# VectorE turns q and k of three more pairs, TensorE masks part of the second batch, and slots no longer go two by two

## The chip, the cores and the metric

One NeuronCore of a Trainium2 chip runs the whole program. The metric is the device time of one execution in microseconds (us): the kernel before takes 1088.77 us, the median of three runs (1088.58 to 1090.57).

## The reference

Two blocks follow each other. First a block-sparse attention over 4 batches, 8 heads, 768 positions, head size 64:

```python
scores = scale * np.matmul(q, k.transpose(0, 1, 3, 2))
# mask in blocks of 32: neighbours, first and last block, and three sampled blocks per row of blocks
scores = np.where(mask, scores, -1000000000.0)
attn = softmax(scores)                  # max subtracted, sum + 1e-9
attn_out = np.matmul(attn, v)           # (B, H, S, D) -> x of (B, S, H*D) = (4, 768, 512)
```

Then a Fourier mixing layer with a channel network (512 to 2048 to 512):

```python
X = np.fft.fft(np.fft.fft(x, axis=1), axis=2)
u = x + np.real(X)
un = (u - mean(u)) / np.sqrt(var(u) + 1e-06)
return u + np.maximum(un @ w_ch1, 0.0) @ w_ch2
```

Everything is fp32.

## The kernel before

**Attention in units and slots.** Heads go in pairs: 16 pairs `n`, four to a batch, `NP = 4`. A pair has two halves of 384 queries and six chunks of 128 keys, so twelve *units* (half, chunk). Two units make a *slot*: six slots to a pair, 24 (`SB`) to a batch, 96 in all. Below, slots are counted from 0, so the second batch has slots 24 to 47.

For a unit, `scores` (L536) multiplies on TensorE (L551): two matmuls of 64 rows, one for each head, into one of two PSUM tiles `s`. In the first batch two more matmuls (L559) add the mask as a product of two bf16 factors, `of_k` and `off_q`. `weigh` (L563) takes the exponential on ScalarE: in the first batch straight from `s` to `e` (L569); later in place in `s` (L572), and VectorE multiplies by a 0/1 mask of bytes on the way to `e` (L574). There are four `e` buffers. From the second batch on GpSimd adds the `e` of a half up in `acc` (L584), from which TensorE makes the softmax sums once per pair (`total`, L677); in the first batch TensorE does it for each slot (`add_up`, L663). `values` (L587) multiplies by v (L597).

**Turning q and k.** Both have to have the head dimension on the partitions. In `turn` (L472) TensorE transposes 12 tiles a pair (L486) and ScalarE copies them out of PSUM (L489, L495). From pair `BY_VECTOR` on, `load_blocks` brings q and k in blocks of 32, VectorE turns them (`flip_blocks`, L520) and ScalarE puts q in order (`in_order`, L528). The loads go through SyncE's queue.

**The mixing layer.** Once a batch has its attention, `begin` (L1251) lines up its steps: `before` and `after`, a long chain of small steps through VectorE (scaling L705, folds L728 to L756, arrivals L855, normalisation L866 to L880), TensorE (`zp`, `pq`, `utp`) and ScalarE, kept in `apart`; and `rest`, the *channels* (`quad` L992 and `channels` L1048), 155.6 us of TensorE work per batch by the planner's numbers, which go to `late` when the chain is through.

**The order.** Each engine runs its instructions in the order in which the program issues them, and the whole order is written by a planner in the program: `when` holds its guess of each engine's time, and `slot` (L1271) issues scores, exponentials, values, then steps of the mixing layer where `gap` (L1215) finds that they would be ready, then channels at a pace that keeps 100 us (`COVER`) of them back for the next batch's chain. The planner sums its own constants (0.9 us for a scaling, for instance), not measured times.

A batch's tiles are reused two batches later, so `until` at slot 53 empties `late` of the first batch before the third batch writes its first result.

When `late` is not empty at an even slot, `paired` is set for good: the sums of two slots are held back in `due`, and the order becomes scores, four units' values, scores, channels.

Of the kernel before, what the change touches and what calls it, by code (L numbers as in the profile page):

```python
# [12 lines left out]
BF16 = mybir.dt.bfloat16  # L13
# [4 lines left out]
ALU = mybir.AluOpType  # L18
# [84 lines left out]
def kernel(  # L103
# [14 lines left out]
    nc = tc.nc  # L118
# [73 lines left out]
    def busy(engine, us, after=0.0):  # L192
        when[engine] = max(when[engine], after) + us
        return when[engine]
# [14 lines left out]
    loaded, v_of = {}, {}  # L209


    BY_VECTOR = 2 * NP + 1

    def load_blocks(n, a, tile):

# [219 lines left out]
    def room(i, shape, name, dtype=FP32):  # L435
        return big.tile(shape, dtype, tag=f"big{i}", name=name)
# [29 lines left out]

    turned, e_of, acc_of, o_of, sums_of, x_of, sp_of = {}, {}, {}, {}, {}, {}, {}
    s_at, e_at, oT_at, acc_at = {}, {}, {}, {}  # L470

# [64 lines left out]
    def scores(us):  # L536

        n, w = divmod(us[0], UP)
        half = w // C
        qT, kT = turned[n, 0], turned[n, 1]  # L540
        queries = slice(half * HS, (half + 1) * HS)
        got = []
        for u in us:
            c = u % C
            s = ps_s.tile([P, 2, 512], FP32, tag="s", name="s")
            got.append((u, s))
            busy("PE", 0.72, max(e_at.get(u - SLOT, 0.0), z_at[u % 2]))
            s_at[u] = when["PE"] + HOP
            for i in range(2):
                rows = slice(D * i, D * i + D)  # L550
                nc.tensor.matmul(s[:, i, 0:HS], kT[rows, c * P:(c + 1) * P], qT[rows, queries],  # L551
                                 start=True, stop=n >= NP)
        for u, s in got if n < NP else ():
            c = u % C
            busy("PE", 0.25)
            s_at[u] = when["PE"] + HOP
            for i in range(2):
                rows = slice(D * i, D * i + D)
                nc.tensor.matmul(s[:, i, 0:HS], of_k[rows, c * P:(c + 1) * P], off_q[rows, queries],  # L559
                                 start=False, stop=True)  # L560
        return got

    def weigh(u, s):  # L563
        n, w = divmod(u, UP)
        half, c = divmod(w, C)
        e = ep.tile([P, 2, HS], FP32, tag="e", name="e")
        e_of[u] = e
        if n < NP:
            nc.scalar.activation(out=e, in_=s[:, :, 0:HS], func=ACT.Exp, scale=scale)  # L569
            e_at[u] = busy("ACT", 0.8, s_at[u]) + HOP  # L570
            return
        nc.scalar.activation(out=s[:, :, 0:HS], in_=s[:, :, 0:HS], func=ACT.Exp, scale=scale)  # L572
        m = mask[:, c, half * HS:(half + 1) * HS].rearrange("p (o s) -> p o s", o=1)
        nc.vector.tensor_tensor(out=e, in0=s[:, :, 0:HS], in1=m.broadcast_to([P, 2, HS]),  # L574
                                op=ALU.mult)
        e_at[u] = busy("DVE", 0.97, busy("ACT", 0.8, s_at[u]) + HOP) + HOP
        if c > 0:
            acc_at[n, half] = busy("POOL", 2.0, e_at[u]) + HOP
        if c == 1:
            acc_of[n, half] = acc_p.tile([P, 2, HS], FP32, tag="acc", name="acc")  # L580

        for i in range(2 if c > 0 else 0):
            acc = acc_of[n, half][:, i, :]
            nc.gpsimd.tensor_add(out=acc, in0=e_of[u - 1][:, i, :] if c == 1 else acc,  # L584
                                 in1=e[:, i, :])
# [601 lines left out]
    SP = UP // SLOT  # L1187
    SB = SP * NP
    W_PACE = 1.42
    short, apart, late, due = deque(), deque(), deque(), deque()  # L1190
    state = {"paired": False, "w": 0, "got": 0, "owed": 0.0, "ready": 0.0}

    def channel_step():
        late.popleft()[0]()
# [20 lines left out]
    def gap(rest=0.0, ahead=None, kinds="tm"):  # L1215

        used = "".join(k for k in "tm" if k not in kinds)
        if ahead is None:
            ahead = AHEAD if late else ALONE
        while apart:  # L1220
            kind, fn, pe, act, dve, need = apart[0]
            if len(late) > need:
                break
            if kind in "dw":
                if kind == "w" and rstd_at[0] > max(when["DVE"], when["PE"]) + 0.2:
                    break
                if max(when["DVE"], state["ready"]) + dve > when["PE"] + rest + ahead:
                    break
            elif kind != "-":
                bank_at = (max if kind == "M" else min)(free[kind.lower()])  # L1230
                if kind.lower() in used or max(state["ready"], bank_at) > when["PE"] + 0.1:
                    break
                used += kind.lower()
            do_apart()
        for item in list(short):
            kind, ready, fn = item
            if kind not in used and max(ready, min(free[kind])) <= when["PE"] + 0.1:
                used += kind
                short.remove(item)
                fn()  # L1240
# [10 lines left out]
    def begin(b):  # L1251


        before, after, rest = mixer(b, x_of[b, 0], x_of[b, 1])
        any_of = len(late) + len(apart) + 4 * len(rest)
        hold = 2 * T
        apart.extend((*step, any_of) for step in norm_steps(b) + before)
        apart.extend((*step, hold) for step in after)
        apart.append(("-", lambda: late.extend(rest), 0.0, 0.0, 0.0, hold))

    def w_loads():
        while state["got"] < min(len(wchunks), state["w"] + ROOMS):
# [3 lines left out]
    def w_steps(sl):  # L1266
        while state["w"] < min(len(wchunks), W_PACE * sl):
            w_round(state["w"])
            state["w"] += 1

    def slot(sl):  # L1271
        phase, r = divmod(sl, SB)
        n, s = divmod(sl, SP)
        units = range(SLOT * sl, SLOT * sl + SLOT)
        opens = sl % 2 == 0
        state["paired"] |= opens and len(late) > 0
        paired = state["paired"]

        def sum_up():

            at = due.popleft()
            done = range(SLOT * at, SLOT * at + SLOT)
            for u in done:
                values(u)
            if at < SB:
                add_up(done)
            for u in done:
                e_of.pop(u)

        if paired and len(due) == 2 and due[0] % SP % T == T - 1:
            sum_up()
        got = scores(units) if sl < B * SB else ()
        if paired and len(due) == 2:
            sum_up()
        for u, ps in got:
            weigh(u, ps)
        if not paired and not late:  # L1300
            gap(1.5)
        while due and (opens or not paired):
            sum_up()
        due.append(sl)
        if s == (4 if paired else 3) and n + 2 < len(pairs):
            load_q(n + 2)
        if s == 0 and 0 < n < len(pairs) - 1:
            load_k(n + 1)

        reuse = n % NP == 0 and phase >= 2  # L1310
        if sl > 0 and s == (5 if reuse else 4 if paired else 3) and sl <= B * SB:
            b, j = pairs[n]
            at = oT_at[n, 0]
            if reuse:
                until(lambda: (b - 2, 0) in finished)
                at = when["PE"] + LEAVES
            if in_blocks(n):
                place_blocks(n, 0)
            else:
                short.append(("t", at, lambda: place(n, 0)))  # L1320
# [12 lines left out]
        if sl > SB and s == 0 and sl <= B * SB:  # L1333
            short.append(("t", acc_at[n - 1, 1], lambda: total(n - 1)))
        if n + 1 < len(pairs):
            for at, a, half in ((1, 0, 0), (2 if n > 0 else 3, 0, 1),
                                (3 if paired else 4, 1, 0), (5, 1, 1)):
                if s == at and n + 1 < BY_VECTOR:
                    short.append(("t", 0.0, lambda a=a, half=half: turn(n + 1, a, half)))
            if s == 1:  # L1340
                load_v(n + 1)
# [9 lines left out]
        us = sum(step[1] for step in late)  # L1351
        pace = max(LEAST, min(MOST, (us - COVER) / left)) if left > 0 else MOST
        state["owed"] = min(state["owed"], pace) + pace if late else 0.0
        more = paired and opens and sl < B * SB
        if not more:
            gap(max(state["owed"], 0.0))
        while not more and late and state["owed"] >= late[0][1] / 2:
            state["owed"] -= late[0][1]
            channel_step()
            gap(max(state["owed"], 0.0))  # L1360

        must = (3, 5) if paired else (2, 5)
        while short and (not more or r == 0) and (s in must or len(short) > 1 or phase == 0 or r == 0):
            ready = [i for i in short if max(i[1], min(free[i[0]])) <= when["PE"] + 0.1]
            if not ready and s not in must and r > 0 and sl > 1:
                break
            item = ready[0] if ready else short[0]
            short.remove(item)
            item[2]()
# [5 lines left out]
                    fn(*args)  # L1375
        w_loads()
        w_steps(sl)
        if sl >= 4 and sl % 2 == 0:
            table_step()

# [139 lines left out]
```

## Time and profile before

| | |
|---|---|
| median of three runs | 1088.77 us |
| the profiled execution | 1088.58 us, of which the span from first to last instruction is 1086.9 us |
| TensorE matmuls | 1046.6 us busy |
| VectorE | 683.2 us |
| ScalarE | 380.1 us |
| GpSimd | 271.0 us |
| granted TensorE clock | 0.992 of full speed, mean |

Lines are those of the kernel as printed above. PE is TensorE's matmul, PEld its weight load, DVE VectorE, ACT ScalarE, POOL GpSimd, SP SyncE; a `q` behind a name is that engine's sequencer. A line of the timeline has the start, the duration, the engine, the line, the operation, what it writes and reads with shapes, the count that was merged, and in brackets how long the engine stood idle before it and who released it. An fp32 matmul leaves two records, so a slot's scores are `x8`. A matmul's duration in the records covers its own pipeline; the step from one start to the next tells better what it costs TensorE.

### The profile page before, as it was taken

Reading aid. Unit: us, or ns where it says so; the run is one execution under the profiler, and the core shown is the slowest. Engines: PE = TensorE matmul, PEld = TensorE weight load, DVE = VectorE, ACT = ScalarE, POOL = GpSimd, SP = SyncE. Lnnn points to the kernel's source line nnn. Section 1 sums busy time; section 2 is a strip of 40 time slices with the busy share of each in tenths; the row PEclk is TensorE's granted clock in tenths of the full one; section 3 lists DMA queues with packets and bytes.
Section 4 is the critical chain, followed back from the end, with each engine's and each line's share of the span. In section 5 each row is a group of like instructions: output and inputs, shape, how many; then the busy total and the mean of one; then the engine's idle time right before and its main releaser. Section 6 shows DMA issues by size and latency. Waiting matters only on the chain.

```text
span 1086.9 us, 12424 instructions
## 1 busy us (share of the span) xinstructions
PE 1046.6 (96%) x4334; PEld 537.4 (49%) x4334; DVE 683.2 (63%) x1241; ACT 380.1 (35%) x762; POOL 271.0 (25%) x302
## 2 busy tenths in 40 slices
PE   8999988988999999999999999999999999999996
PEld 4333333543555545444444545454444555568575
DVE  5899878498754525665568535664556355575663
ACT  5988655555212102353342202344330202220210
POOL 1000177678000001246546000344630001000000
PEclk9999999999999999999999999999999999999999
DMA  7757211022000000222211000211000001000001
GB/s 223 225 168 238 82 45 44 15 49 41 0 1 1 0 1 19 68 38 42 54 26 33 1 1 10 59 42 37 15 8 8 1 1 29 30 1 1 1 17 45
DMA packets 108194, 46.66 MB, mean 43 GB/s; under 512 B 95822, under 2 KB 100956, under 8 KB 108124
## 3 DMA queue, kind: packets, MB, share of 16 engines
q1 hardware_dynamic: 106236, 44.99, 16.4%
q10 hardware_dynamic: 1856, 0.79, 0.3%
q8 instruction: 36, 0.59, 0.2%
q14 instruction: 34, 0.28, 0.1%
q0 software_dynamic: 32, 0.01, 0.0%
HBM read 37.11 MB, written 6.29 MB: 40 GB/s over the span
## 4 chain that ended last, share of the span: by engine, by line
PE 84%; DVE 10%; issue 2%; ACT 2%; POOL 1%; DMA 0%; ACTq 0%; DVEq 0%; POOLq 0%
PE y L1048 22%; PE z L992 15%; PE s L551 10%; PE o L597 9%; PE yp L992 8%; PE yy L1111 6%; PE xp L992 4%; DVE e L574 3%; PE zp L805 2%; PE sp L663 1%; PE zp L776 1%; DVE t L954 1%; PE tp L486 1%; DVE x L855 1%; POOL acc L584 1%
## 5 line engine op out<-in xcount | busy, mean ns | idle before, releaser
L584 POOL TENSOR_TENSOR acc<-acc,e 128x384 f32<-128x384 f32 x192 | 196.3, 1055 | 72.2 <-DVE e L574 71.9
L574 DVE TENSOR_TENSOR e<-s,mask 128x768 f32<-128x768 f32 x144 | 131.2, 949 | 70.3 <-ACT s L572 62.2
L551 PE MATMUL s<-qT,kT 64*128 64x384 f32 x768 | 157.6, 524 | 12.5 <-DVE e L574 10.9
L572 ACT ACTIVATE s<-s 128x768 f32<-128x768 f32 x144 | 110.0, 793 | 107.3 <-PE s L551 106.5
L597 PE MATMUL o<-e,vr 128*64 128x384 f32 x768 | 143.5, 501 | 0.0
L1048 PE MATMUL y<-w_sb,hA 128*128 128x512 f32 x288 | 129.0, 595 | 1.1 <-ACT zs L807 1.1
L1048 PE MATMUL y<-w_sb,hB 128*128 128x512 f32 x288 | 128.5, 596 | 1.0 <-DVE x L1051 1.0
L1051 DVE TENSOR_TENSOR x<-y,x 128x512 f32<-128x512 f32 x72 | 49.7, 691 | 125.4 <-PE y L1048 125.2
L584 POOL TENSOR_TENSOR acc<-e 128x384 f32<-128x384 f32 x48 | 51.2, 1088 | 223.2 <-DVE e L574 137.6
L551 PEld LDWEIGHTS s<-qT,kT 64*128 64x128 f32 x768 | 63.8, 187 | 86.7 <-DVE e L574 39.2
L868 POOL TENSOR_SCALAR st<-st 128x1 f32<-128x1 f32 x24 | 6.6, 276 | 351.8 <-DVE st L867 351.4
L992 PE MATMUL z<-unT,t 128*128 128x384 f32 x256 | 93.0, 486 | 0.0
L997 DVE TENSOR_TENSOR hA<-z,hA 128x384 f32<-128x384 f32 x64 | 35.7, 558 | 86.1 <-PE z L992 86.1
L1048 PEld LDWEIGHTS y<-w_sb,hB 128*128 128x128 f32 x288 | 53.4, 190 | 67.7 <-issue 64.6
L597 PEld LDWEIGHTS o<-e,vr 128*64 128x64 f32 x768 | 48.2, 137 | 75.2 <-issue 72.2
L1048 PEld LDWEIGHTS y<-w_sb,hA 128*128 128x128 f32 x288 | 53.1, 190 | 64.2 <-issue 58.0
L1001 ACT ACTIVATE hA<-hA 128x384 f32<-128x384 f32 x64 | 33.5, 523 | 120.8 <-DVE hA L997 120.6
L992 PEld LDWEIGHTS z<-unT,t 128*128 128x128 f32 x256 | 48.6, 190 | 33.9
L1001 ACT ACTIVATE hB<-hB 128x384 f32<-128x384 f32 x64 | 33.5, 523 | 86.0 <-DVE hB L997 86.0
L992 PE MATMUL xp<-unT,w_sb 128*128 128x384 f32 x128 | 48.9, 505 | 3.1 <-DVE x L1051 2.6
L1012 ACT COPY hA<-xp 128x384 f32<-128x384 f32 x32 | 15.3, 479 | 99.0 <-PE xp L992 99.0
L992 PE MATMUL yp<-unT,w_sb 128*128 128x384 f32 x128 | 47.0, 490 | 0.4 <-DVE un L841 0.4
(200 smaller groups left out, 1398.0 us busy)
## 6 DMA issues: line engine op xcount, KB each, us to landing
wraw<-in_moe_w_ch_dram SPq DMA_DIRECT2D x32, 512.0 KB
vr<-in_v_dram SPq DMA_DIRECT2D x30, 192.0 KB
qr<-in_q_dram SPq DMA_DIRECT2D x48, 64.0 KB
x<-oT SPq DMA_DIRECT2D x192, 12.0 KB
kr<-in_k_dram SPq DMA_DIRECT2D x14, 192.0 KB
qb<-in_q_dram SPq DMA_DIRECT2D x28, 96.0 KB
kb<-in_k_dram SPq DMA_DIRECT2D x28, 96.0 KB
out_dram<-x SPq DMA_DIRECT2D x16, 128.0 KB
```

The costliest lines, as they stand in the source:

```text
L551: nc.tensor.matmul(s[:, i, 0:HS], kT[rows, c * P:(c + 1) * P], qT[rows, queries], start=True, stop=n >= NP)
L572: nc.scalar.activation(out=s[:, :, 0:HS], in_=s[:, :, 0:HS], func=ACT.Exp, scale=scale)
L574: nc.vector.tensor_tensor(out=e, in0=s[:, :, 0:HS], in1=m.broadcast_to([P, 2, HS]), op=ALU.mult)
L584: nc.gpsimd.tensor_add(out=acc, in0=e_of[u - 1][:, i, :] if c == 1 else acc, in1=e[:, i, :])
L597: nc.tensor.matmul(o[D * i:D * i + D, :], vt[:, i, c, :], e[:, i, :], start=(c == 0), stop=(c == C - 1))
L805: nc.tensor.matmul(ps[:, 0:KS - 1], sd[:, t, parts[g - 2]], sn_sb[:, t, :], start=(t == 0), stop=(t == T - 1))
L992: nc.tensor.matmul(to, a[:, k, :], c[:, k, :], start=(k == 0), stop=(k == ND // 2 - 1))
L997: tt(out=to, in0=ps, in1=a, op=ALU.add)
L1001: nc.scalar.activation(out=h, in_=h, func=ACT.Relu)
L1048: nc.tensor.matmul(y, hs[0, half][:, l, m * P:(m + 1) * P], w2_sb[:, 4 * r + l, :], start=(l == 0), stop=(l == 3))
L1051: nc.vector.tensor_tensor(out=x[:, m, :], in0=y, in1=x[:, m, :], op=ALU.add)
L1111: nc.tensor.matmul(ps, a[:, k, :], c[k // 2][:, k % 2, :] if isinstance(c, list) else c[:, k, :], start=(k == 0), stop=(k == 3))
```

## The change

1. `BY_VECTOR` falls from `2 * NP + 1` to `NP + 1`: VectorE turns q and k of pairs 5 to 8 too (pairs from 9 on already went this way).
2. The two bf16 factors are copied at slot 21 (`SB - 3`) into a free buffer by two DMAs. While that copy is there, units of the second batch are masked by TensorE as in the first batch: two more matmuls each, exponential straight into `e`, no multiplication on VectorE. GpSimd still adds `e` up. When the first batch's channels go to `late`, the copy is given up, and from then on VectorE masks.
3. The pairing of slots is taken out: every slot issues scores, exponentials, the previous slot's values, and then steps of the mixing layer and channels.

```diff
-    BY_VECTOR = 2 * NP + 1
+    BY_VECTOR = NP + 1
...
+    by_pe = set()
+    factors = {"at": (of_k, off_q)}
+    def keep_factors():
+        kept = room(2, [P, 2, S], "factors", BF16)
+        for a, t in enumerate(factors["at"]):
+            nc.sync.dma_start(out=kept[:, a, :], in_=t)
+        factors["at"] = kept[:, 0, :], kept[:, 1, :]
...
+            if n < NP or (factors["at"] and True):
+                by_pe.add(u)
...
-        for u, s in got if n < NP else ():
+        for u, s in got:
+            if u not in by_pe:
+                continue
+            c, (at_k, at_q) = u % C, factors["at"]
...
-        if n < NP:
+        if u in by_pe:
             nc.scalar.activation(out=e, in_=s[:, :, 0:HS], func=ACT.Exp, scale=scale)
+        else:
+            nc.scalar.activation(out=s[:, :, 0:HS], in_=s[:, :, 0:HS], func=ACT.Exp, scale=scale)
+            nc.vector.tensor_tensor(out=e, in0=s[:, :, 0:HS], in1=m.broadcast_to([P, 2, HS]),
...
+        def go():
+            late.extend(rest)
+            factors["at"] = None
+        apart.append(("-", go, 0.0, 0.0, 0.0, hold))
...
-        if paired and len(due) == 2 and due[0] % SP % T == T - 1:
-            sum_up()
-        got = scores(units) if sl < B * SB else ()
-        if paired and len(due) == 2:
-            sum_up()
-        for u, ps in got:
-            weigh(u, ps)
-        if not paired and not late:
-            gap(1.5)
-        while due and (opens or not paired):
-            sum_up()
-        due.append(sl)
+        if sl < B * SB:
+            for u, ps in scores(units):
+                weigh(u, ps)
+        if not late:
+            gap(1.5)
+        if 0 < sl <= B * SB:
+            done = [u - SLOT for u in units]
+            for u in done:
+                values(u)
...
-        more = paired and opens and sl < B * SB
-        if not more:
-            gap(max(state["owed"], 0.0))
-        while not more and late and state["owed"] >= late[0][1] / 2:
+        gap(max(state["owed"], 0.0))
+        while late and state["owed"] >= late[0][1] / 2:
...
+        if sl == SB - 3:
+            keep_factors()
```

In the paired order some steps came one slot later (q's load and the first half's placing at the fifth slot of a pair instead of the fourth, one turning at the fourth instead of the fifth); these go back too.

More of the change, by code (lines that the diff above doesn't have):

```diff
@@ L551, in scores @@
                 nc.tensor.matmul(s[:, i, 0:HS], kT[rows, c * P:(c + 1) * P], qT[rows, queries],
-                                 start=True, stop=n >= NP)
-        for u, s in got if n < NP else ():
-            c = u % C
+                                 start=True, stop=u not in by_pe)
+        for u, s in got:
+            if u not in by_pe:
+                continue
+            c, (at_k, at_q) = u % C, factors["at"]
             busy("PE", 0.25)
@@ L558, in scores @@
                 rows = slice(D * i, D * i + D)
-                nc.tensor.matmul(s[:, i, 0:HS], of_k[rows, c * P:(c + 1) * P], off_q[rows, queries],
+                nc.tensor.matmul(s[:, i, 0:HS], at_k[rows, c * P:(c + 1) * P], at_q[rows, queries],
                                  start=False, stop=True)
@@ L567, in weigh @@
         e_of[u] = e
-        if n < NP:
+        if u in by_pe:
             nc.scalar.activation(out=e, in_=s[:, :, 0:HS], func=ACT.Exp, scale=scale)
             e_at[u] = busy("ACT", 0.8, s_at[u]) + HOP
-            return
[L572 to L576, printed above, removed]
+        else:
+            nc.scalar.activation(out=s[:, :, 0:HS], in_=s[:, :, 0:HS], func=ACT.Exp, scale=scale)
+            m = mask[:, c, half * HS:(half + 1) * HS].rearrange("p (o s) -> p o s", o=1)
+            nc.vector.tensor_tensor(out=e, in0=s[:, :, 0:HS], in1=m.broadcast_to([P, 2, HS]),
+                                    op=ALU.mult)
+            e_at[u] = busy("DVE", 0.97, busy("ACT", 0.8, s_at[u]) + HOP) + HOP
+        if n < NP:
+            return
         if c > 0:
@@ L1189 @@
     W_PACE = 1.42
-    short, apart, late, due = deque(), deque(), deque(), deque()
-    state = {"paired": False, "w": 0, "got": 0, "owed": 0.0, "ready": 0.0}
+    short, apart, late = deque(), deque(), deque()
+    state = {"w": 0, "got": 0, "owed": 0.0, "ready": 0.0}
     def channel_step():
@@ L1258, in begin @@
         apart.extend((*step, hold) for step in after)
-        apart.append(("-", lambda: late.extend(rest), 0.0, 0.0, 0.0, hold))
+        def go():
+            late.extend(rest)
+            factors["at"] = None
+        apart.append(("-", go, 0.0, 0.0, 0.0, hold))
     def w_loads():
@@ L1274, in slot @@
         units = range(SLOT * sl, SLOT * sl + SLOT)
[L1275 to L1282, printed above, removed]
+        if sl < B * SB:
[5 more added lines that the diff above has]
+            done = [u - SLOT for u in units]
             for u in done:
                 values(u)
-            if at < SB:
+            if phase == 0 or sl == SB:
                 add_up(done)
@@ L1288, in sum_up @@
                 e_of.pop(u)
-        if paired and len(due) == 2 and due[0] % SP % T == T - 1:
-            sum_up()
-        got = scores(units) if sl < B * SB else ()
-        if paired and len(due) == 2:
-            sum_up()
-        for u, ps in got:
-            weigh(u, ps)
-        if not paired and not late:
-            gap(1.5)
-        while due and (opens or not paired):
-            sum_up()
-        due.append(sl)
-        if s == (4 if paired else 3) and n + 2 < len(pairs):
+        if s == 3 and n + 2 < len(pairs):
             load_q(n + 2)
@@ L1310, in slot @@
         reuse = n % NP == 0 and phase >= 2
-        if sl > 0 and s == (5 if reuse else 4 if paired else 3) and sl <= B * SB:
+        if sl > 0 and s == (5 if reuse else 3) and sl <= B * SB:
             b, j = pairs[n]
@@ L1335, in slot @@
         if n + 1 < len(pairs):
-            for at, a, half in ((1, 0, 0), (2 if n > 0 else 3, 0, 1),
-                                (3 if paired else 4, 1, 0), (5, 1, 1)):
+            for at, a, half in ((1, 0, 0), (2 if n > 0 else 3, 0, 1), (4, 1, 0), (5, 1, 1)):
                 if s == at and n + 1 < BY_VECTOR:
@@ L1360, in slot @@
             gap(max(state["owed"], 0.0))
-        must = (3, 5) if paired else (2, 5)
-        while short and (not more or r == 0) and (s in must or len(short) > 1 or phase == 0 or r == 0):
+        while short and (s in (2, 5) or len(short) > 1 or phase == 0 or r == 0):
             ready = [i for i in short if max(i[1], min(free[i[0]])) <= when["PE"] + 0.1]
-            if not ready and s not in must and r > 0 and sl > 1:
+            if not ready and s not in (2, 5) and r > 0 and sl > 1:
                 break
```

## The prediction, made before the change was run

> **What bounds the kernel now.** First the page's busy times, then busy times by stretch.
>
> ```profile
> PE 1046.6 (96%) x4334; PEld 537.4 (49%) x4334; DVE 683.2 (63%) x1241; ACT 380.1 (35%) x762; POOL 271.0 (25%) x302
> ```
> ```profile
> 123.00:271.30 148.30, 130.75 (x700) 56.92 (x699) 113.27 (x157) 81.77 (x170) 108.74 (x111) 0.96 0.18 41
> 271.30:438.00 166.70, 165.16 (x493) 87.54 (x493) 88.03 (x180) 28.33 (x60) 8.12 (x14) 0.99 0.02 5
> 438.00:583.00 145.00, 143.44 (x610) 63.98 (x608) 93.84 (x128) 61.38 (x113) 73.52 (x74) 1.00 0.24 47
> ```
>
> The columns are stretch, length, then busy us (records) of PE, PEld, DVE, ACT, POOL, then the granted clock. PE bounds nearly everything, but from 123.0 us (slot 24, the second batch's first) to 271.3 us (the first channels, after slot 53's scores) it idles 17.5 us and the clock is 0.96. In this stretch the first batch's chain of mixing steps runs, with no channels to fill in. The timeline of PE there:
>
> ```profile
> 129.56 2.23 PE L551 MATMUL s<-qT,kT 64*128 64x384 f32 x8 [2.25 <-DVE e L574]
> 131.71 2.71 PE L597 MATMUL o<-e,vr 128*64 128x384 f32 x8
> ...
> 141.50 2.93 PE L551 MATMUL s<-qT,kT 64*128 64x384 f32 x8
> ```
>
> Scores wait until VectorE has multiplied an earlier unit and so freed `s`; after a wait values take 2.71 us and scores 2.93, against 1.51 and 1.56 elsewhere. The waits of the stretch (total us, times, longest):
>
> ```profile
> PEld s L551 <- DVE e L574: 23.5, 28, 3.2
> ...
> POOL acc L584 <- PE sp L677: 13.5, 4, 9.3
> ```
>
> What PE needs there, by steps from start to start: 30 slots of scores 1.49 and values 1.44, 87.9; placings 9 x 0.48, 4.3; sums 4 x 0.78 + 0.78, 3.9; turnings of four pairs at 0.58 + 0.37 + 2 x 0.48, 7.6; the mixing layer's st 1.0, zp 9.2, pq 4.7, utp 3.1. Together 121.7 of 148.3: **26.6 us are lost to waits and a slow clock**. The same reckoning finds 2 to 3 us lost in each of the later attention stretches. So once channels exist time is PE's work, and before that it is waits on VectorE.
>
> **The factors.** A first-batch slot shows their price:
>
> ```profile
> 108.99 1.56 PE L551 MATMUL s<-qT,kT 64*128 64x384 f32 x8
> 110.39 0.49 PE L559 MATMUL s<-at_q,at_k 64*128 64x384 bf16 x4
> 110.81 1.51 PE L597 MATMUL o<-e,vr 128*64 128x384 f32 x8
> ```
>
> 0.42 us a slot (110.39 to 110.81). Off VectorE go two multiplications of 0.95. For how many slots? The chain from slot 25 to the channels is some 45 us of VectorE (a quarter of its rows among the groups by line is 42, and GpSimd's adds stretch it), 17 of PE and 10 of ScalarE, one after another, 72 us; a slot without VectorE in its path is 2.93 + 0.42 of PE and about 0.8 of placings, sums and chain, 4.2. 72/4.2 is 17 slots, so channels come at slot 42, not 53, and 18 slots (24 to 41) carry factors: **+7.6 us** (30 slots would be 12.6). VectorE loses 36 x 0.95 = 34 us. The scores' wait for the multiplication becomes one for the exponential: 0.82 against 0.79 + 0.95. A new wait: ScalarE writes `e` itself, so where GpSimd is late with its sums, the exponential stands, behind it the copies of `oT`, `xt` and `q`, and PE behind those. Before, VectorE met that wait in this stretch three times for 2.4 us; it is in the remainder below. The two copying DMAs at slot 21 (about 110 us) stand on SP's queue behind weight loads; its next load in before is issued at 124.49, so nothing behind them is late. They cost nothing unless they land after 123, when slot 24 would stand.
>
> **Turning pairs 5 to 8 on VectorE.** PE: **-7.6 us**, as counted. VectorE gains 4 x (0.97 + 1.52) = 10 us. ScalarE loses two copies of 0.48 and nine of 0.24 a pair and gains six of 0.31. SP issues four q loads (2.05 us) for six (3.82) and four k loads (2.10) for two (1.23). In before a k load issued at 485.42 has left the DMA engines by about 492, and a turn comes four slots after its load, 17 us: covered, and in the other case a few us of waiting in VectorE's queue, with the chain's steps behind it.
>
> **What stays of the 26.6 us.** Two rows say that not all goes. The chain is planned at 0.9 us a scaling and shorter folds than it takes beside GpSimd:
>
> ```profile
> 139.60 0.69 DVE L705 TENSOR_TENSOR x<-x,r 128x512 f32<-128x512 f32 x1
> ...
> 149.48 3.94 DVE L705 TENSOR_TENSOR x<-x,r 128x512 f32<-128x512 f32 x3
> ```
>
> 0.69 alone, 1.31 each while GpSimd adds (its own adds stretch from 1.0 to 1.3). In before, scalings and folds between 139 and 187 us sum to 21.1 us; with a pair's turning (2.5) and a sum (0.5) that is 24.1. The planner reckons 6 x 0.9 + 9.6 + 2.0 = 17.0. With no masks between, PE arrives at the first `zp` when the planner says, some 7 us early, and stands. For pq and utp, which came with 9.8 us of loss in before (191.9 to 271.3), I take half, 5. So **12 us stay, 14.6 go**. Ends: 4, a little under 6 (0.34 a slot, the rate from 191.9 to 243.7, over 18 slots), as no mask is in the path any more; and 18, if the folds' 7 come with 1 of slow clock and all of the 9.8 stays.
>
> The Trainium skill ("SBUF — State Buffer", section "SBUF: two separate sides") says that GpSimd and a VectorE operation with two SBUF inputs take the shared port pair in turns, and the loser blocks for a whole instruction. The rows show a slowdown of that kind, 0.69 to 1.31, but not all of it. If it held for every pair of operations, GpSimd's 63 us of adds in 18 slots and VectorE's 30 us of two-input steps would make 93 us where PE has 76 to 84; my estimate of what stays would then be 21, not 12, and the gain gone.
>
> **Unpairing.** The third batch in before:
>
> ```profile
> 462.38 1.56 PE L551 MATMUL s<-qT,kT 64*128 64x384 f32 x8
> 463.87 2.80 PE L597 MATMUL o<-e,vr 128*64 128x384 f32 x16
> 466.60 1.56 PE L551 MATMUL s<-qT,kT 64*128 64x384 f32 x8
> 468.09 1.51 PE L597 MATMUL o<-e,vr 128*64 128x384 f32 x8
> 469.53 1.72 PE L551 MATMUL s<-qT,kT 64*128 64x384 f32 x8
> 471.18 1.51 PE L597 MATMUL o<-e,vr 128*64 128x384 f32 x8
> ```
>
> Four units' values step 2.73 us, two times two would 2.88: 0.15 saved, 14 times in slots 54 to 95, **2.1 us** lost. A run of channels costs 0.19 more than its parts (x16: 7.06 against 2 x 3.44); two to four more runs, 0.8. The scores at 469.53 step 1.65 against 1.49: with no channels between, a slot catches VectorE's second multiplication (0.75 + 0.79 + 2 x 0.95 = 3.44 us after a slot's start, where PE wants it at 2.93 + 0.75 = 3.68, so any other VectorE step spoils it). At the planned 2.9 us of channels a slot, some 16 of the 42 slots will have none; before had seven such a batch too. I take 2. Together **5 us**, between 3 and 10.
>
> The Trainium skill ("TensorEngine Tiling (Array Packing)", section "Tiling Modes") says that a change of tiling mode drains TensorE. It speaks against this part; the 0.15 us above is what the trace shows of it, and no more is counted.
>
> **Channels earlier.** Some ten runs of channels now stand among slots 42 to 52 where they stood in a row: 10 x 0.19 = **1.9 us**.
>
> **Sum.** 14.6 + 7.6 - 7.6 - 5 - 1.9 = 7.7 us off the profiled execution's 1088.6: 1080.9, say **1081**. The median lies 0.2 above that execution, which changes nothing.
>
> **Rivals.** A, slower: *unpaired slots wait for VectorE.* In the second batch unpaired slots with no channels lost 26.6/30 = 0.9 us each. If the 16 such slots of the third and fourth batch do too, unpairing costs 14.4 + 2.9 = 17 us, and 1081 becomes 1093. It decides from about 0.6 us a slot, (7.7 + 2)/16. For it: turnings of 1.5 us and x additions of 0.7 sit in that queue. Against: the 0.16 above, and that VectorE's long folds come in other slots. B: *the change doesn't bring channels earlier.* The planner still needs until slot 53, so 30 slots pay 12.6 for factors and all that goes is waits: 1081 + 5 - 1.9, 1084; half of the scatter around that is no difference. C: *hardly any wait stays* (4 us): 1073.
>
> **Chances.** Forecast 0.55 (its own range 1075 to 1087), C 0.10, B 0.15, A 0.20. 0.2% is 2.2 us, about what a measurement of this kernel can tell from no change: 1086.6 and 1091.0 are the limits. Faster: 0.53 of the forecast, 0.10 of C, 0.06 of B, 0.69. Same: 0.02 + 0.09 of B + 0.01 of A, 0.12. Slower 0.19, all of A. The range goes from C, with a little beyond it, to the lower part of A, 1072 to 1091; above it lies some 0.13.
>
> **What would show it.** Right: L559 has 96 + 72 records or near it; scores waits on L574 before the first channel row are gone; that row comes near 215 us; L486 falls by 48 records; losses before it shrink to about 12 us, with a wait at the first `zp`; L597 shows `x8` only, and scores between two values step 1.5 to 1.7. Wrong: over 100 records more on L559 (B), waits of a us on L574 in channel-less slots after 438 us (A), or a long stand of ScalarE's exponential for GpSimd.

## The result, and the profile after

The kernel after takes **1117.78 us**, median of four runs (1116.60 to 1119.03). Against 1088.67 us for the kernel before, timed beside it, that is a ratio of 1.0264 with a 95% interval of 1.0247 to 1.0282: 29 us slower, where 8 us faster was forecast. The profiled execution took 1117.41 us, its span is 1115.7 us, and the mean granted clock fell from 0.992 to 0.983.

The busy times of the page, then busy times by stretch (columns as in the prediction): slot 24 to the first channels, from there to slot 54, and a stretch of the fourth batch.

```profile
PE 1052.4 (94%) x4370; PEld 535.0 (48%) x4370; DVE 666.4 (60%) x1207; ACT 375.4 (34%) x742; POOL 278.6 (25%) x302
```
```profile
127.94:242.70 114.76, 98.08 (x576) 45.96 (x576) 66.88 (x99) 57.88 (x112) 79.26 (x79) 0.93 0.20 39
242.70:446.36 203.66, 196.71 (x659) 98.14 (x657) 113.35 (x203) 48.10 (x99) 42.53 (x46) 0.99 0.06 12
...
700.00:763.00 63.00, 50.05 (x240) 20.26 (x240) 46.02 (x65) 27.14 (x51) 39.87 (x44) 0.95 0.24 52
```

PE's records are those of the change: 4334, plus 84 for the factors, less 48 turnings, is 4370. The first channels come 28.6 us earlier, at 242.70 instead of 271.29. But PE idles 16.7 us before them, 7 us in the stretch behind them, and 13 us of the 63 after 700 us, where in before it was busy for 61.2 of 63.

With PE's time reckoned as in the prediction, by normal steps from start to start, this is what waits and a slow clock take in each stretch:

| stretch | before | after | difference |
|---|---|---|---|
| 9 us to slot 24's scores (123.05 / 127.94) | 1.1 | 6.2 | +5.1 |
| to the first channels (271.29 / 242.70) | 27.0 | 20.5 | -6.5 |
| to slot 54's scores (438.83 / 446.36) | 1.7 | 9.6 | +7.9 |
| to 700 us | 3.2 | 7.7 | +4.5 |
| 700 to 763 us | 2.0 | 16.4 | +14.4 |
| 763 to 960 us | 3.0 | 3.8 | +0.8 |

Together +26.2 us of the 28.8 by which the span grew; the other 2.6 are PE's own work. So it is waits, with the slow clock behind them, that made the change slow. The large ones stand in PE's timeline (in brackets, how long it stood and for whom):

```profile
118.23 0.50 PE L575 MATMUL s<-factors 64*128 64x384 bf16 x4 [3.55 <-DMA factors<-at_q]
...
159.02 2.93 PE L565 MATMUL s<-qT,kT 64*128 64x384 f32 x8 [8.78 <-DVE kT L532]
...
217.68 1.12 PE L935 MATMUL utp<-ident,un 128*128 128x128 f32 x4 [6.27 <-DVE sums L665]
...
726.75 1.11 PE L935 MATMUL utp<-ident,un 128*128 128x128 f32 x4 [7.00 <-ACT x L638]
...
752.29 1.78 PE L565 MATMUL s<-qT,kT 64*128 64x384 f32 x8 [3.10 <-DVE e L590]
```

The first four are followed back here; the last, in the same stretch as the fourth, was not.

**118.23, the copy.** The chain of waits shows the DMAs that copy the factors:

```profile
113.55 0.53 SPq L478
114.12 4.07 DMA factors<-at_q
118.23 0.50 PE s L575 x4
```

The copy is issued in slot 21, but `factors["at"]` points at it at once, so the very next slot, 22, already reads it, and PE is at that slot's factors 0.6 us after the second issue. The groups by line agree: the last two slots of the first batch are among the users of the copy (92 records, 23 slots; the original is left with 88 instead of 96).

```profile
L575 PE MATMUL s<-factors x92: 319/323/524, 118.2 to 240.4; 64*128 64x384 bf16 x92
...
L575 PE MATMUL s<-at_q,at_k x88: 322/322/323, 10.0 to 110.2; 64*128 64x384 bf16 x88
```

**159.02, keys turned by VectorE.** VectorE's timeline before this wait, and GpSimd's beside it:

```profile
139.78 7.87 DVE L723 TENSOR_TENSOR x<-x,r 128x512 f32<-128x512 f32 x6
...
152.51 1.74 DVE L750 TENSOR_TENSOR sa<-sa 128x765 f32<-128x765 f32 x1
154.17 1.21 DVE L757 TENSOR_TENSOR e<-x 128x255 f32<-128x255 f32 x1
155.30 0.95 DVE L758 COPY e<-x 128x2 f32<-128x2 f32 x1
156.29 1.17 DVE L759 SCALAR_TENSOR_TENSOR e<-e,flip,sa 128x257 f32<-128x257 f32 x1
157.38 1.49 DVE L532 STREAM_TRANSPOSE kT<-kb 128x768 f32<-128x768 f32 x1
```
```profile
147.06 12.21 POOL L602 TENSOR_TENSOR acc<-acc,e 128x384 f32<-128x384 f32 x8
```

The turning itself takes 1.5 us; ahead of it VectorE has worked without a pause since 139.29 on scalings and folds. Those are slow in a way that says something: a copy of two columns takes 0.95 us here.

**217.68, a stand of GpSimd.** TensorE's `utp` goes to a PSUM buffer that a sum (L665) has to be read out of first. That sum stands in VectorE's order behind the chain's normalisation, and so does the turning of the next q, for which ScalarE stands 7.1 us. Slow instructions are the smaller part of it here: two additions of L873 take 2.34 us (0.76 four us later, when GpSimd is idle). Before them VectorE stood for 8.1 us. One step of the normalisation (L888) is GpSimd's, and in GpSimd's order it comes behind the first additions of a pair, which stood for TensorE's sums of the pair before (`sp`, L695):

```profile
206.62 1.95 POOL L602 TENSOR_TENSOR acc<-e 128x384 f32<-128x384 f32 x2 [7.83 <-PE sp L695]
...
209.57 1.21 DVE L898 TENSOR_SCALAR un<-x,st 128x512 f32<-128x512 f32 x1 [8.12 <-POOL st L888]
```

TensorE's order has these sums behind the scores of slot 38. In two of the runs below, the factors alone and the factors without pairing, they come behind slot 36's; there VectorE stands 2.0 us at this place, and TensorE does not stand at `utp`. ScalarE's exponential stood 4.2 us for GpSimd at the same place (208.60), the new wait that the prediction had named.

**726.75, channels run out.** ScalarE's timeline and the chain of waits:

```profile
726.22 0.48 ACT L638 COPY x<-xt 128x384 f32<-128x384 f32 x1 [9.73 <-DMA out_dram<-x]
```
```profile
713.71 0.70 DVE x L1069
714.43 11.62 DMA out_dram<-x
```

ScalarE puts a piece of the fourth batch in a tile that the second batch's last result has just left (11.6 us to land; SP issues five stores in a row there). It stands 9.7 us, and the exponentials, `q` and `unT` behind it stand too. In before no such copy between 690 and 800 us waits for a store. Here the program's own order has no channels left from slot 80 to slot 89, while the third batch's chain is under way.

### The profile page after: what moved, and what is told of

Its sections match the earlier page's. It is cut to its first block, busy times and chain, and to the rows that moved or that the text cites. A ratio compares the mean times of both kernels' runs of the same rounds, so it can differ in the third digit from the quotient of the medians.

```text
span 1115.7 us, 12397 instructions
## 1 busy us (share of the span) xinstructions
PE 1052.4 (94%) x4370; PEld 535.0 (48%) x4370; DVE 666.4 (60%) x1207; ACT 375.4 (34%) x742; POOL 278.6 (25%) x302
## 4 chain that ended last, share of the span: by engine, by line
PE 83%; DVE 8%; DMA 3%; ACT 2%; SPq 2%; issue 2%; POOL 0%; DVEq 0%; ACTq 0%; POOLq 0%
PE y L1066 22%; PE z L1010 15%; PE s L565 10%; PE o L615 9%; PE yp L1010 7%; PE yy L1129 6%; PE xp L1010 4%; SPq L653 2%; PE zp L823 1%; DVE x L723 1%; DMA out_dram<-x 1%; PE sp L681 1%; PE s L575 1%; PE zp L794 1%; DVE e L590 1%
## 5 line engine op out<-in xcount | busy, mean ns | idle before, releaser
L602 POOL TENSOR_TENSOR acc<-acc,e 128x384 f32<-128x384 f32 x192 | 204.6, 1099 | 99.8 <-DVE e L590 91.1
L615 PE MATMUL o<-e,vr 128*64 128x384 f32 x768 | 150.2, 514 | 2.2 <-DVE oT L622 2.2
L590 DVE TENSOR_TENSOR e<-s,mask 128x768 f32<-128x768 f32 x102 | 92.6, 947 | 50.5 <-ACT s L588 49.5
L588 ACT ACTIVATE s<-s 128x768 f32<-128x768 f32 x102 | 77.3, 790 | 127.9 <-PE s L565 127.1
L585 ACT ACTIVATE e<-s 128x768 f32<-128x768 f32 x90 | 68.1, 813 | 32.7 <-PE s L575 28.3
L1010 PE MATMUL z<-t,w_sb 128*128 128x384 f32 x128 | 46.8, 488 | 1.9 <-DVE t L972 1.9
```

What stands on the lines that cost most here:

```text
L615: nc.tensor.matmul(o[D * i:D * i + D, :], vt[:, i, c, :], e[:, i, :], start=(c == 0), stop=(c == C - 1))
L1010: nc.tensor.matmul(to, a[:, k, :], c[:, k, :], start=(k == 0), stop=(k == ND // 2 - 1))
```

## The experiments

The first four take the change apart. Theory S: the three parts each have a fault of their own, unpairing the largest. Theory J: the loss is joint; channels that start earlier leave too few to cover the third batch's chain.

**Pairing kept, the two other parts made** (pairing only had to begin at another slot than the fifth of a pair):

```diff
-        state["paired"] |= opens and len(late) > 0
+        state["paired"] |= opens and s != 4 and len(late) > 0
```

> The kernel before with the first two parts of the change (VectorE turns pairs 5 to 8, factors until channels), the pairing of slots kept (it may start at the first or third slot of a pair). Theory S (separate faults: the copied factors are used before they have landed, 5 us; the chain before the channels still makes TensorE wait, so those two parts gain nothing there, +2.6; the rest of the loss, 21 us, belongs to unpairing): 1096 us, between 1093 and 1099, with no long stand of ScalarE for out_dram in the fourth batch. Theory J (joint: channels that start earlier leave too few of them to cover the third batch's chain, and the stand near 714 us comes from that): the stand is there with pairing too, about 1110.

**Unpairing alone**, on the kernel before:

```diff
-        state["paired"] |= opens and len(late) > 0
+        state["paired"] = False
```

> The kernel before with nothing but the pairing taken out. S: 1110 us (1104 to 1112), with ScalarE's copy of the fourth batch's first result (L620) standing 8 us or more for out_dram. J: only merged values and single waits for the mask are lost, 1091 to 1096, and no such stand.

**VectorE's turning alone**, on the kernel before:

```diff
-    BY_VECTOR = 2 * NP + 1
+    BY_VECTOR = NP + 1
```

> The kernel before with BY_VECTOR = NP + 1 alone. S: TensorE's 7.6 us of turnings lie in a stretch that waits for VectorE, and VectorE gets 10 us more to do there: between 1086 and 1094, scores waiting for kT about as e1. J says the same. If turning on VectorE were a clear gain by itself: 1081.

**The factors alone**, on the kernel before (the diff's `by_pe`, `factors`, `keep_factors` and `go`):

> The kernel before with the factors alone, pairs 5 to 8 turned by TensorE, slots paired. S: 5 us for the copy, 9 for the factors, the wait for kT (8.8) not there, but waits at the first zp instead: 1092 to 1098. If the wait for kT is a loss of its own that does not move to zp: 1086 to 1090.

| kernel | us | ratio, 95% interval |
|---|---|---|
| pairing kept, other two | 1092.45 | 1.0034 [1.0022, 1.0046] |
| unpairing alone | 1092.91 | 1.0038 [1.0027, 1.0048] |
| VectorE's turning alone | 1100.82 | 1.0113 [1.0096, 1.0130] |
| factors alone | 1085.52 | 0.9966 [0.9954, 0.9979] |

Unpairing costs 4.5 us against the 1088.38 timed beside it, where S had 22, and ScalarE's copy stands 2.7 us for a store, not 9.7: S falls. The three parts add up to +14.0 (4.5 + 12.4 - 2.9), so 15 of the 29 us are joint. But J's number for the first run is missed too: channels start at 242.66 there, as in after, and there is no stand. An early start is not enough. Two more numbers were missed: VectorE's turning alone took 7 us more than the 1094 up to which both theories went, and the factors alone came out below all that was expected of them. In the run with VectorE's turning alone, scores wait longer for masks that now share VectorE's queue with the turnings (123 to 280 us; 23.5 in before, up to 271.3):

```profile
PEld s L551 <- DVE e L574: 36.2, 33, 4.9
```

**Where the channels run out.** The program's own lists were printed for each kernel. They are empty in slots 80 to 89 in after, and in none of the four parts. The difference shows in slots 77 to 80. In after, 18 entries of `late` are left at slot 77 and 0 at slot 80, with 19 steps of the chain to go. With unpairing alone there are 19 at slot 77, the chain's first `zp` gets in 11 us earlier, and at slot 80 the chain is through and `late` holds 32 new ones. Theory K: this gap is the joint loss. Theory U: unpaired slots lose wherever they stand. Two runs with `COVER` changed, after without the gap and unpairing alone with it:

```diff
-    COVER = 100.0
+    COVER = 105.0      # the kernel after
...
+    COVER = 95.0       # unpairing alone
```

> The changed kernel with COVER = 105 for 100 and nothing else. By the program's own order, in the changed kernel the second batch's channels run out ten slots (80 to 89) before the third batch's chain is through; with 105 they don't. Theory K (that gap without channels, set off by the three parts together, is the loss that no part shows alone, some 17 us): 1098 to 1102 us, no stand for out_dram near 714. Theory U (unpaired slots lose time everywhere once channels come early): 1112 to 1118, only the stand moves.

> The kernel before with the pairing taken out (e2, 1092.9 us) and COVER = 95. By the program's own order this brings the same gap without channels in slots 80 to 89 as in the changed kernel, with neither factors nor more turning on VectorE. K: 1092.9 + 17, 1106 to 1113. U: 1092 to 1096.

Unpairing alone with `COVER` 95 took 1112.80 us (1.0216 [1.0192, 1.0240]), 20 us more than with 100, with neither factors nor VectorE's turning in it. PE's timeline of it shows after's stands, nearly to the tenth:

```profile
716.43 1.12 PE L917 MATMUL utp<-ident,un 128*128 128x128 f32 x4 [7.06 <-ACT x L620]
...
741.94 2.93 PE L551 MATMUL s<-qT,kT 64*128 64x384 f32 x8 [3.10 <-DVE e L574]
```

That is for K. But after with `COVER` 105 took 1113.76 us (1.0231 [1.0214, 1.0248]), not 1098 to 1102: the stand at 700 us was gone, as K says, but the time is in U's range. A new stand had come: channels wait for `hA`, which stands in VectorE's order behind a chain's scalings, and those had stood 2.9 us for a transfer:

```profile
579.28 1.90 DVE L723 TENSOR_TENSOR x<-x,r 128x512 f32<-128x512 f32 x3 [2.94 <-DMA x<-oT]
...
581.70 2.92 PE L1010 MATMUL z<-unT,t 128*128 128x384 f32 x4 [4.99 <-DVE hA L1015]
```

So either the loss moves about (theory W), or 105 moved one thing too many. `COVER` 102 fills the gap too, and leaves the order in slots 77 to 80 as it is with unpairing alone:

> The kernel after with COVER 102 instead of 100: in the program's own order there are channels left in every slot from 45 to the end, and the counts in slots 77 to 80 are those of the run with the pairing alone taken out. K: the stand of 16 us between 700 and 763 us goes and nothing takes its place, 1117.8 - 16 = 1102, between 1099 and 1105. W: the loss comes back at another place, as with cover 105, 1110 to 1115.

It took 1104.55 us (1.0138 [1.0121, 1.0155]), 13.2 less than after. Busy times of the stretch in which after stood:

```profile
690.00:763.00 73.00, 70.60 (x282) 31.80 (x283) 40.95 (x67) 27.12 (x50) 27.52 (x31) 0.98 0.22 47
```

PE is busy for 70.6 of 73 us. The gap is worth 13 us here (20 in unpairing alone), and W falls as a general rule; the collision of the run with 105 is that run's own.

**Do unpairing and factors add up without VectorE's turning?**

> The kernel before with the pairing taken out and with the factors in the second batch, but ScalarE and TensorE still turning pairs 5 to 8. The program's own order has channels waiting in every slot from 43 on, so no gap in slots 80 to 89. If the gap is what makes the three parts cost more together than alone (theory K), this pair of parts adds up: 1088.7 + 4.5 - 2.9 = 1090, between 1087 and 1094. If the unpaired order loses whenever channels come early (theory W: VectorE's work for the channels collides with a chain's scalings wherever the two meet), it takes 1100 or more without any gap, with waits of z for hA as in the run with cover 105.

They do: 1087.36 us (0.9990 [0.9975, 1.0005]), at the low end of K's 1087 to 1094, with no gap. In its timeline PE's one long stand in the chain is 3.65 us for the first `zp`:

```profile
158.66 2.02 PE L792 MATMUL zp<-cs_sb,sa 128*128 128x385 f32 x4 [3.65 <-DVE sa L765]
```

The step from here to after is VectorE's turning of pairs 5 to 8 and nothing else, and it costs 30.4 us: 13.2 are the gap that it brings about, 17 are not.

**Is VectorE's queue long because GpSimd adds beside it?** In after, four of the five additions of each half (chunks 2 to 5) are left out in the slots of the second batch that TensorE masks:

```diff
-        for i in range(2 if c > 0 else 0):
+        for i in range((2 if c == 1 or u not in by_pe else 0) if c > 0 else 0):
```

> The kernel after without GpSimd's sums of chunks 2 to 5 in the slots of the second batch that TensorE masks (the softmax sums of that batch lack four of six chunks; order and all else as in after). It asks whether VectorE's scalings and folds are slow there because GpSimd adds beside them. If so, a scaling takes about 0.7 us where it took 1.31, kT of the pair in work is turned some 5 us earlier, the wait of 8.8 us at 159 us falls under 4, and the first channels come 5 to 10 us before 242.7. If VectorE's queue is full by itself, scalings still take 1.2 or more and the wait stays at 7 to 9 us.

This kernel's softmax sums are incomplete; it only asks for time. It was timed once: 1099.95 us, 17.8 below after. VectorE's timeline and PE's, to be held against 139.78, 155.30 and 159.02 above:

```profile
139.55 3.70 DVE L723 TENSOR_TENSOR x<-x,r 128x512 f32<-128x512 f32 x6
...
148.99 0.41 DVE L757 TENSOR_TENSOR e<-x 128x255 f32<-128x255 f32 x1
149.33 0.15 DVE L758 COPY e<-x 128x2 f32<-128x2 f32 x1
149.52 0.49 DVE L759 SCALAR_TENSOR_TENSOR e<-e,flip,sa 128x257 f32<-128x257 f32 x1
149.92 1.48 DVE L532 STREAM_TRANSPOSE kT<-kb 128x768 f32<-128x768 f32 x1
```
```profile
151.54 1.56 PE L565 MATMUL s<-qT,kT 64*128 64x384 f32 x8 [1.52 <-DVE kT L532]
```

The same instructions in the same order: a scaling takes 0.62 instead of 1.31 us, keys are turned 7.5 us earlier, PE waits 1.5 us instead of 8.8, and the first channels come at 229.25. So this wait is due to the additions. The wait at `utp` is so only in part: VectorE's stand for GpSimd before it is again 8.1 us, as the first addition of each half still waits for the sums, and PE waits 3.9 us there instead of 6.3. Lost time between slot 24 and the channels is 7.9 us instead of 20.5. The gap after 700 us stays (15.9 lost from 700 to 750).

**Does it help to turn that pair's keys earlier?** With pairing kept and both other parts, pair 5's `kT` is turned two slots earlier, before the scalings:

```diff
-                                 (2, in_order, (n + 1,)), (4, flip_blocks, (n + 1, 1)),
+                                 (2 if n == NP else 4, flip_blocks, (n + 1, 1)), (2, in_order, (n + 1,)),
```

> The paired kernel with both other parts (e1, 1092.5 us), where only pair 5's k is turned two slots earlier, ahead of the chain's scalings and folds in VectorE's order. If the wait of 8.8 us for kT is a loss by itself: 1082 to 1085. If it moves to the first zp, which stands behind the same folds: 1089 to 1092, with a wait of 4 to 6 us on VectorE at zp.

No: 1093.54 us (1.0035 [1.0020, 1.0049]) against 1092.45 without it. The wait has only gone to the chain's own result:

```profile
162.62 2.94 PE L792 MATMUL zp<-cs_sb,sa 128*128 128x385 f32 x4 [7.11 <-DVE sa L765]
```

VectorE has that much to do there; the order of it changes who waits.

**The early use of the copy**, undone in after, and in the factors alone (the copy is taken into use at slot 24):

```diff
-        factors["at"] = kept[:, 0, :], kept[:, 1, :]
+        factors["kept"] = kept[:, 0, :], kept[:, 1, :]
...
+        if sl == SB - 1:
+            factors["at"] = factors["kept"]
```

> The kernel after, with the copied factors used from slot 24 on instead of from slot 22 on, nothing else. If the early use of the copy is a loss of its own, as it was with the factors alone (7 us), slot 24's scores come 4.9 us earlier, as in before, and the whole takes 1117.8 - 5 to 7, 1111 to 1113; the gap in slots 80 to 89 stays. If the wait is hidden by the later waits for VectorE (the chain begins at the same time), the kernel takes 1116 to 1118.

> The factors alone (as e4, 1085.5 us), with the copied factors used from slot 24 on and the originals in slots 22 and 23. K, with the copy's landing as a loss of its own (3.3 us of waiting and 1.3 of slow clock at slot 22): 1080 to 1082, lower than both kernels. If what was lost there only moves to the chain's next wait (the first zp, 3.6 us in e4): 1084 to 1086.

In after it is worth 4.3 us (1113.53 us, 1.0228 [1.0209, 1.0246]). With the factors alone it is worth 7.0, and that kernel is **the fastest of all: 1078.54 us, 0.9903 [0.9886, 0.9919]** against before, with pairing and TensorE's turnings as they were. Its page shows PE busy for 97% of a shorter span:

```profile
PE 1044.8 (97%) x4410; PEld 539.9 (50%) x4410; DVE 655.9 (61%) x1203; ACT 379.0 (35%) x762; POOL 272.6 (25%) x302
```

## Why the prediction was wrong

**What held.** What bounds the kernel was read rightly. Factors cost 0.42 us a slot in 21 slots, 8.8 us against 7.6 forecast. Unpairing alone cost 4.5 against 5, and the same run refutes rival A, which had 17 us for it. The whole came out slower, as A had it, but not for A's reason. B falls with the early channels. C, hardly any wait stays (4 us), is near for the factors alone (7 us) and far for the whole. Channels did come earlier, at slot 45 and not 42, at 242.7 and not 215 us. PE's work came to 2.6 us more, where the sum's terms gave 4.8 (7.6 - 7.6 + 2.1 + 0.8 + 1.9). All that went wrong is waits: +26.2 us instead of -12.6 (14.6 gone, 2 for unpaired slots).

**"12 us stay, 14.6 go": 20.5 stay.** Of the steps that stand in the sum this failed by most, and the error lies in what I charged VectorE's turning with. I put its 2.5 us a pair into the sum of scalings and folds and made PE wait at the first `zp` alone, for 7 us. But a turning is on the way to the *scores*: at 159.02 it stood in VectorE's order behind 17.6 us of chain, and the slot that needs it has nothing else to run. Up to 164.7 us, behind that slot, about 10.6 us are lost. The 5 us put down for `pq` and `utp` came to about 9.8, most of it around the stand of GpSimd before 217.68. Without VectorE's turning, the lost time between slot 24 and the channels was 7.4 us with unpairing (6.8 without), so 12 was even cautious for the factors. With it, 20.5. I had also written that a turn "comes four slots after its load, 17 us: covered", which looks at the load; the wait in VectorE's queue stands there as the other case, with "a few us" and no term in the sum. The 7.6 us that TensorE was to gain by it were never seen: VectorE's turning cost 12.4 us alone, 6.9 with the factors and pairing (1092.45 less 1085.52), and 30.4 with the factors and without pairing.

**The 1.31 us of a scaling.** The prediction took 21.1 us of scalings and folds over from before's rows; in after they come to 22.2, so this term was nearly right, and it was used in the wrong place. How the time arises it left open. Side by side, after and the run with fewer additions show a price for each instruction: 0.41 to 1.21, 0.15 to 0.95, 0.49 to 1.17, 0.62 to 1.31, so 0.7 to 0.8 us whether it moves two columns or 512. The large fold pays it as well; the run with fewer additions does not show this, as it has two additions beside that fold, but after's last chain does, where GpSimd has no more additions:

```profile
147.68 2.44 DVE L746 TENSOR_TENSOR sa<-x 128x1536 f32<-128x1536 f32 x1
...
856.10 1.76 DVE L746 TENSOR_TENSOR sa<-x 128x1536 f32<-128x1536 f32 x1
```

The row that the prediction calls alone, 0.69 at 139.60 in before, has GpSimd adding on both sides of it; there it was the addition that began 0.1 us later which took 1.40 instead of 0.99. The Trainium skill ("SBUF — State Buffer", section "SBUF: two separate sides") has a VectorE operation with two SBUF inputs, or in a two-port mode, and a GpSimd operation shut each other out of the shared ports, each for a whole instruction. A price that does not grow with size agrees with that. The estimate made from that rule, 21 us that stay, was set aside for 12, and 20.5 were measured. That it came so near is partly luck, as without the turnings 7 stayed beside the same additions.

**The copy, "nothing unless it lands after 123".** It landed at 118.2 and cost 4.3 us. The step assumed a first use in slot 24; the code's assignment takes effect at once. Reading which slot is the first with `factors["at"]` changed would have shown it.

**The gap after 700 us: in no step.** 13.2 us, by the run with `COVER` 102. The prediction costed pairing by its local prices, and treated the order elsewhere as given. The order is worked out by the program from its own guesses, and a small shift in slot 77 leaves ten slots without channels. Unpairing alone with `COVER` 95 shows the same stand, so neither the factors nor VectorE's turning is needed for it, and unpairing alone with 100 and after with 102 do without it: it is an alignment that the change happened to meet. Every kernel here that has it is unpaired; no paired one was run with another `COVER`. Its lists do not depend on the chip, and would have shown it.

**The rest.** From the first channels to 700 us after loses 12.4 us more than before, of which the prediction had 2. The rows show channels that wait for `hA` while VectorE scales beside GpSimd (2.12 us at 321 us) and single waits of 1.7 us for masks. With unpairing and factors alone the stretch from 300 to 350 us loses 0.9, after 7.1, so VectorE's turning, or the later channels that come with it, has a part in it. Which of these does it was not tried apart, and the cause of this part stays open.

By size, in the reckoning of the table: 14.4 of the gap, 8.1 (14.6 less 6.5) of what stayed before the channels, 10.4 (12.4 less 2) of what was lost behind them, 5.1 before slot 24, 0.8 at the end, less 2.2 of PE's work, is 36.6 us; the span grew by 28.8 where 7.7 were to go, 36.5.

## What to carry to other kernels

Before work is moved to an engine that is "only 60% busy", look at its queue in the stretch where the moved result is needed: here 1.5 us of turning waited behind 17.6 us of a chain, and that one wait of TensorE, 8.8 us, was more than the 7.6 us that it got rid of. When an order is made by a planner, print what the planner does with the change over the whole run before costing it by rows; a gap may open 500 us away. And when a copied operand is switched in, find the first reader: it may be the next one, not the one it was made for.

## What the runs showed of the hardware

Beside GpSimd's additions of 128x384 fp32, VectorE's additions, scalings and copies from SBUF to SBUF took 0.7 to 0.8 us more each in the chain between 139 and 158 us, from 128x2 (0.15 to 0.95) to 128x765 (0.94 to 1.74), and a fold of 128x1536 took 2.44 instead of 1.76. Other instructions took no more: a transposition of 128x768 (1.49 and 1.48), a reciprocal of 128x48 (0.45 at 139.29 beside additions, 0.45 at 139.06 in the run with fewer, GpSimd idle), and two multiplications by the mask, which read PSUM (1.79 at 736.68 beside additions, 1.82 at 729.28 with GpSimd idle). The additions stretched as well, from 0.98 us each (1.96 for two) to 1.53 (12.21 for eight). A copy of two bf16 tensors of 128x768 within SBUF took 4.1 us from its second issue until its reader could start, and the store of one tile, the last of five issued in a row, 11.6 us from its data to its landing.
